# Order on a full TensorE: single score rounds, grouped head turns, later last values and new load estimates in a fused attention and mixer kernel

## The chip, the cores and the metric

The kernel runs on one core of one Trainium2 chip. The metric is the time of one execution on the device in microseconds; the profile's span is about 1.8 us shorter than the time of the same execution. A verdict calls 2% a difference. All comparisons below are between runs in the fast state, unless said otherwise. The granted clock is the share of TensorE's full clock that the trace shows as granted.

## The reference, cut to what matters

```python
def _attn_ref(q, k, v):                                   # 8 x 12 x 448 x 64 each
    scores = scale * np.matmul(q, k.transpose(0, 1, 3, 2)) - np.log(S)
    attn = 1.0 / (1.0 + np.exp(-scores))                  # sigmoid, no row sums
    return np.matmul(attn, v)

def _moe_ref(x, w_tok1, w_tok2, w_ch1, w_ch2):            # x: 8 x 448 x 768
    h = np.maximum(x.transpose(0, 2, 1) @ w_tok1, 0.0) @ w_tok2      # token mixing
    u = x + h.transpose(0, 2, 1)
    return u + np.maximum(u @ w_ch1, 0.0) @ w_ch2                    # channel mixing
```

Heads are handled in pairs of pairs: batch b has three groups m of four heads. The names in the trace are: `tk`, `tq` (the "turn", a transpose on TensorE), `qk` (a score round), `xa` (values), `xb` (turn back to x), `k` and `yn` (the two token products), `ut` (row transposes for the channel mix), `c` (the two channel products).

## The kernel before: the parts that matter

The kernel holds a small list scheduler in Python. Each piece of work is an `Op` with an engine and an estimated duration; the scheduler plays the whole program through with these estimates and emits instructions in the order it found. So a changed constant of it changes no instruction, only the order on each engine, and each engine then works through its list, and waits where an operand isn't there (at 24.44 us TensorE waited 1.06 us for a load).

```python
# the wide PSUM buffers for scores: two. The last values of batch 0 hold one of them too.
ps = plan.buf("wide", 2, [128, 2, 512], FP32, "psum", f"qk_{b}_{m}_{i}_{hs[0]}")
...
# score rounds are emitted in visits to TensorE, two rounds in each; the values of a head
# group join the fifth and the eighth visit, the last ones form a visit of their own
parts = [rs[i : i + 2] for i in range(0, len(rs), 2)]
parts[4].append(vs[0])
parts[7].append(vs[1])
groups += [(b, i / len(parts), g) for i, g in enumerate(parts)]
groups.append((b, 1.0, [vs[-1]]))
...
# when a visit is due, in us of mixer work done
return -1.0 if b < 2 else base[b - 1] - LEAD + i * SPAN * mix[b - 1]
...
# turns of batches 0 and 1 (later batches turn by DMA): one operation per head, seven
# transposes, each head into its own half of the partitions
for h in hs:
    def turn(ps=ps, h=h):
        for i, j in enumerate(ORDER[side]):
            nc.tensor.transpose(out=ps[64 * h : 64 * h + 64, i, :, :],
                                in_=raw[:, h, j, :], identity=ident[:, :])
...
# when the scheduler thinks that a load lands
free["POOL"] = 1.3
slow = 1.0 if self.pipe > 8.0 else 1.5
self.pipe = max(self.pipe, free["POOL"] + 1.5) + slow * o.us
```

From batch 2 on, x is turned by a transposing DMA: values, two copies on ScalarE, two transposing loads, then the token product of that batch. The rows of u go the same way to the channel product.

## Time and profile before

| | before |
|---|---|
| time, median (3 runs) | 384.69 us (384.46 to 387.5) |
| span of the traced run | 383.8 us |
| TensorE busy | 373.1 us, 97% |
| ScalarE / VectorE busy | 206.8 / 161.0 us |
| first channel product of batch 0 starts | 43.97 us |
| score rounds of batch 1 before it | 4 |

The prediction below shows the lines and reads them.

### The profile page before, as it was taken

What the parts mean: (1) busy time and instruction counts of PE and PEld (TensorE: products, weight loads), DVE (VectorE), ACT (ScalarE), POOL (GpSimd) and SP (SyncE); (2) the same over time, 40 slices, a digit from 0 to 9 for tenths busy, and PEclk for the clock granted to TensorE, in tenths of its full rate; (3) what the DMA queues carried; (4) which work ended last, traced back from release to release, by engine and by line L of the source; (5) the groups of instructions that cost most, each with busy time, mean ns of one, the idle gap of its engine ahead of it and who ended that gap; (6) DMA issues with size and microseconds to landing.
All of it is one profiled execution on the core that took longest, in us unless ns stands there. A gap on an engine that the chain in (4) does not pass through costs nothing.

```text
span 383.8 us, 7923 instructions
## 1 busy us (share of the span) xinstructions
PE 373.1 (97%) x3240; PEld 193.1 (50%) x3240; DVE 161.0 (42%) x296; ACT 206.8 (54%) x252; POOL 118.6 (31%) x265
## 2 busy tenths in 40 slices
PE   8989999998999999999999999999999999999995
PEld 4545544554444554444455554444445565555663
DVE  3345535355335413552341334633522264754221
ACT  2986676559757764686555665975564420200000
POOL 9973127453345423433443334344000000000000
PEclk9999999999999999999999999999999999999999
DMA  6999999979987999699797999998214463300343
GB/s 78 179 175 205 208 209 155 173 116 156 151 131 115 174 187 206 96 144 182 114 139 136 178 184 193 125 189 121 40 28 100 101 134 85 72 2 0 84 118 87
DMA packets 98804, 50.56 MB, mean 132 GB/s; under 512 B 72336, under 2 KB 95120, under 8 KB 98768
## 3 DMA queue, kind: packets, MB, share of 16 engines
q0 software_dynamic: 24400, 21.93, 42.1%
q1 hardware_dynamic: 74368, 28.13, 39.4%
q8 instruction: 25, 0.41, 0.4%
q14 instruction: 11, 0.09, 0.1%
HBM read 43.84 MB, written 11.01 MB: 143 GB/s over the span
## 4 chain that ended last, share of the span: by engine, by line
PE 87%; DMA 6%; POOL 3%; ACT 2%; DVE 1%; issue 1%; SPq 0%; POOLq 0%; ACTq 0%
PE c L861 29%; PE c L906 24%; PE qk L532 9%; PE xa L569 8%; PE yn L784 5%; PE k L754 5%; PE c L915 3%; DMA k<-in_k_dram 3%; DMA uT<-u 1%; DMA x<-xT 1%; POOL k L295 1%; POOL q L295 1%; PE k L654 1%; ACT attn L547 1%; POOL w_tok L328 1%
## 5 line engine op out<-in xcount | busy, mean ns | idle before, releaser
L547 ACT ACTIVATE attn<-qk,att_bias 128x896 f16<-128x896 f32 (+1 forms) x172 | 161.8, 988 | 75.1 <-PE qk L532 74.8
L861 PE MATMUL c<-uT,w_ch 128*128 128x448 f16 x576 | 118.1, 353 | 0.8 <-DVE uT L835 0.4
L906 PE MATMUL c<-w_ch,h2aT 128*128 128x384 f16 x576 | 98.8, 326 | 0.0
L886 DVE TENSOR_SCALAR h2aT<-c 128x448 f16<-128x448 f32 x96 | 60.0, 625 | 81.9 <-PE c L861 81.6
L861 PEld LDWEIGHTS <-w_ch 128*128 128x128 f16 x576 | 53.3, 98 | 58.0 <-issue 13.2
L906 PEld LDWEIGHTS <-h2aT 128*128 128x128 f16 x576 | 54.9, 98 | 40.9 <-issue 5.8
L930 DVE TENSOR_TENSOR u<-u,c 128x384 f32<-128x384 f32 x48 | 26.6, 555 | 79.5 <-PE c L906 79.5
L532 PE MATMUL qk<-qT,kT 64*64 64x448 f16 x672 | 52.2, 362 | 0.1
L718 POOL COPY mark<-attn 1x1 f16<-1x1 f16 x54 | 9.7, 180 | 102.9 <-ACT attn L547 102.7
L569 PE MATMUL xa<-attn,v 64*64 64x448 f16 x672 | 37.0, 351 | 0.0
L602 ACT ACTIVATE xT<-xa 128x448 f16<-128x448 f32 x43 | 21.1, 546 | 18.5 <-PE xa L569 18.0
L813 ACT ACTIVATE u<-u 128x768 f16<-128x768 f32 x21 | 17.8, 845 | 20.9 <-DVE u L805 20.8
L532 PEld LDWEIGHTS <-kT 64*64 64x64 f16 x672 | 14.5, 104 | 28.2 <-issue 24.8
L805 DVE TENSOR_TENSOR u<-x,yn 128x384 f32<-128x384 f16 x48 | 24.5, 549 | 9.9 <-PE yn L784 8.2
L784 PE MATMUL yn<-h,w_tok 128*128 128x384 f16 x128 | 26.2, 327 | 0.0
L466 POOL COPY kp<-k 128x384 f16<-128x384 f16 (+1 forms) x54 | 21.3, 431 | 14.0 <-DMA k<-in_k_dram 14.0
L569 PEld LDWEIGHTS <-v 64*64 64x64 f16 x672 | 18.7, 107 | 13.5 <-DMA q<-in_q_dram 1.5
L466 POOL COPY qp<-q 128x384 f16<-128x384 f16 (+1 forms) x54 | 21.4, 434 | 7.5 <-DMA q<-in_q_dram 7.3
L754 PE MATMUL k<-x,w_tok 128*128 128x384 f16 x112 | 20.2, 327 | 0.4 <-DMA x<-xT 0.4
L766 DVE TENSOR_SCALAR h<-k 128x384 f16<-128x384 f32 x28 | 15.6, 557 | 6.0 <-PE k L754 4.6
L784 PEld LDWEIGHTS <-w_tok 128*128 128x128 f16 x128 | 11.2, 98 | 11.7 <-issue 4.9
L306 POOL DMA_DIRECT2D k<-in_k_dram x21 | 15.1, 719 | 6.2 <-issue 5.6
(57 smaller groups left out, 192.4 us busy)
## 6 DMA issues: line engine op xcount, KB each, us to landing
out_dram<-u SPq DMA_DIRECT2D x48, 192.0 KB, 3.0
k<-in_k_dram POOLq DMA_DIRECT2D x21, 224.0 KB, 5.1
q<-in_q_dram POOLq DMA_DIRECT2D x21, 224.0 KB, 5.4
v<-in_v_dram POOLq DMA_DIRECT2D x21, 224.0 KB, 5.0
w_ch<-in_moe_w_ch_dram POOLq DMA_DIRECT2D x6, 768.0 KB, 16.2
out_dram<-ut SPq DMA_DIRECT2D x8, 192.0 KB, 3.0
v<-in_v_dram POOLq DMA_DIRECT2D x6, 112.0 KB, 4.8
x<-xT SPq DMA_TRANSPOSE x36, 4.1
```

The source lines that it names most:

```text
L466: nc.gpsimd.tensor_copy(out=pm[:, to, :, :], in_=src[:, fr, :, :])
L532: nc.tensor.matmul(out=ps[64 * s : 64 * s + 64, h, 0:S], lhsT=kT[64 * h : 64 * h + 64, i, s, :], rhs=qT[64 * h : 64 * h + 64, :, s, :], st ...
L547: nc.scalar.activation(out=at[:, hs, :], in_=ps[:, hs, 0:S], func=SIGMOID, bias=bias_t[:, :], scale=att_scale,)
L569: nc.tensor.matmul(out=ps[s](slice(64 * h, 64 * h + 64)), lhsT=vf[64 * s : 64 * s + 64, h, order[i], :], rhs=attn[i][64 * s : 64 * s + 64, ...
L602: nc.scalar.activation(out=xt[:, s, c0 : c0 + S], in_=ps[s](every), func=COPYF)
L754: nc.tensor.matmul(out=ps[:, :], lhsT=w_tok1[:, w1_slot(side, blk), 128 * t : 128 * t + 128], rhs=X[b][:, x_block(side, blk), c], start=(b ...
L784: nc.tensor.matmul(out=ps[:, :], lhsT=w_tok2[:, t, s0 : s0 + 2, :], rhs=h1[b][:, t, c], start=(t == 0), stop=(t == 1),)
L805: nc.vector.tensor_tensor(out=to, in0=x, in1=y, op=ADD)
L861: nc.tensor.matmul(out=to(), lhsT=w_ch1[cb // 4][:, db, 128 * (cb % 4) : 128 * (cb % 4) + 128], rhs=uT[b][:, db, :], start=(db == 0), stop ...
L886: nc.vector.tensor_scalar(out=h2aT[b][:, cb, :], in0=to(), scalar1=0.0, scalar2=None, op0=MAX)
L906: nc.tensor.matmul(out=ps[:, :], lhsT=h2aT[b][:, cb, 128 * blk : 128 * blk + 128], rhs=w, start=(cb == 0), stop=(cb == NCB - 1),)
L930: nc.vector.tensor_tensor(out=t, in0=t, in1=ps[:, :], op=ADD)
```

## The change

Its words are: batch 1's score rounds go one by one, not in twos; first turns in halves with heads side by side; last values of a batch join the next batch's visits. The diff also moves `LEAD` and three constants of the load model, and with the new turns the scheduler's estimate of them: 0.32 us for each head before, 0.455 for the two halves together now.

```diff
-        free["POOL"] = 1.3
+        free["POOL"] = 0.8
...
-                slow = 1.0 if self.pipe > 8.0 else 1.5
-                self.pipe = max(self.pipe, free["POOL"] + 1.5) + slow * o.us
+                slow = 1.7 if 9.0 < self.pipe < 13.0 else 1.0
+                self.pipe = max(self.pipe, free["POOL"] + 1.3) + slow * o.us
...
-    LEAD, SPAN, REST, WIDE = 12.0, 0.86, 1.0, 2
+    LEAD, SPAN, REST, WIDE = 16.0, 0.86, 1.0, 2
...
-            for h in hs:
-                def turn(ps=ps, h=h):
-                    for i, j in enumerate(ORDER[side]):
+            for a, z in ((0, 4), (4, J)):
+                def turn(ps=ps, hs=hs, a=a, z=z):
+                    for i in range(a, z):
+                        for h in hs:
...
+                if b == 1:
+                    parts = [[o] for g in parts for o in g]
+                if b >= 4:
+                    parts[1].append(left)
+                left = vs[-1]
...
-            groups.append((b, 1.0, [vs[-1]]))
+            if b == B - 1 or b < 4 - 1:
+                groups.append((b, 1.0, [vs[-1]]))
```

(A `narrow` switch in the choice of buffers is cut: it stays on, and excludes only a third wide buffer that doesn't exist.)

More of the change, by code (lines that the diff above doesn't have):

```diff
@@ L63, in __init__ @@
         self.log, self.kept = [], {}
+        self.narrow = True
         self.far, self.load_far, self.sp_wait = 4.5, 2.0, 2.0
@@ L100, in ready @@
             o = next(iter(new.values()))
-            got = sorted(
-                x for x in (self.slot_time(held, o) for held in self.slots[tag]) if x is not None
-            )
+            got = sorted(x for x, _ in self.free_slots(tag, o))
             if len(got) < len(new):
@@ L107, in ready, with free_slots @@
         return t
+    def free_slots(self, tag, o):
+        got = []
+        for i, held in enumerate(self.slots[tag]):
+            x = self.slot_time(held, o)
+            if tag == "bank" and i > 1 and not self.narrow or tag == "wide" and i == 2 and self.narrow:
+                continue
+            if tag == "wide" and i == 2 and held is None:
+                y = [self.slot_time(h, o) for h in self.slots["bank"][2:]]
+                x = None if None in y else max(y)
+            if x is not None:
+                got.append((x, i))
+        return got
     def hold(self, o):
@@ L111, in hold @@
             if b.slot is None:
-                times = [
-                    (x, i)
-                    for i, held in enumerate(self.slots[b.tag])
-                    if (x := self.slot_time(held, o)) is not None
-                ]
+                times = self.free_slots(b.tag, o)
                 b.slot = min(times)[1]
@@ L484, in turned @@
             parts = []
-            for h in hs:
-                def turn(ps=ps, h=h):
-                    for i, j in enumerate(ORDER[side]):
-                        nc.tensor.transpose(
-                            out=ps[64 * h : 64 * h + 64, i, :, :],
-                            in_=raw[:, h, j, :],
-                            identity=ident[:, :],
-                        )
-                need = [lds[h]] if len(lds) > 1 else lds
-                o = op(f"turn{what}_{b}_{m}_{h}", "PE", 0.32, turn, [*need, ident_op, *hold], [raw, ps, ident, t])
+            for a, z in ((0, 4), (4, J)):
+                def turn(ps=ps, hs=hs, a=a, z=z):
+                    for i in range(a, z):
+                        for h in hs:
+                            nc.tensor.transpose(
+                                out=ps[64 * h : 64 * h + 64, i, :, :],
+                                in_=raw[:, h, ORDER[side][i], :],
+                                identity=ident[:, :],
+                            )
+                need = [lds[hs[0]]] if len(lds) > 1 else lds
+                o = op(f"turn{what}_{b}_{m}_{hs[0]}{a}", "PE", (z - a) * 0.065, turn, [*need, ident_op, *hold], [raw, ps, ident, t])
                 o.pri = 0 if b == 0 else 2.5
```

## The prediction

> **What bounds the kernel now.** I read the busy shares first, then TensorE's timeline (start, duration, engine, instruction, count; a bracket is idle time before it and its releaser), ScalarE's timeline, and the table of waits.
>
> ```profile
> PE 373.1 (97%) x3240; PEld 193.1 (50%) x3240; DVE 161.0 (42%) x296; ACT 206.8 (54%) x252; POOL 118.6 (31%) x265
> ```
>
> TensorE is busy 97% of a 383.8 us span; nothing else passes 54%. Taken at its word, only some 10 us could be won. But "busy" here hides two things, so I went on to starts.
>
> ```profile
> 46.85 2.44 PE L861 MATMUL c<-uT,w_ch 128*128 128x448 f16 x12
> 49.22 0.57 PE L532 MATMUL qk<-qT,kT 64*64 64x448 f16 x8
> 49.73 2.44 PE L861 MATMUL c<-uT,w_ch 128*128 128x448 f16 x12
> ...
> 69.75 0.38 PE L532 MATMUL qk<-qT,kT 64*64 64x448 f16 x4
> 70.06 2.12 PE L906 MATMUL c<-w_ch,h2aT 128*128 128x384 f16 x12
> ...
> 109.38 3.58 PE L861 MATMUL c<-uT,w_ch 128*128 128x448 f16 x18
> 112.89 0.57 PE L532 MATMUL qk<-qT,kT 64*64 64x448 f16 x8
> ```
>
> The first hidden thing is the change of tile shape. From start to next start, 12 channel matmuls take 2.37 us (46.85 to 49.22) and 18 take 3.51; the difference is 0.19 us each, so a run of them carries about 0.1 us beside its matmuls. Two score rounds (x8) take 0.51, one (x4) 0.31: 0.20 a round and 0.11 fixed. Going to the 64*64 shape and back thus costs about 0.22 us, all of it inside "busy".
>
> ```profile
> 5.36 0.83 PE L443 MATMUL idle<-uT 128*128 128x256 f16 x6
> 6.12 0.58 PE L489 MATMUL tq<-ident,q 128*64 128x128 f16 x7
> ...
> 24.44 0.58 PE L489 MATMUL tk<-ident,k 128*64 128x128 f16 x7 [1.06 <-DMA k<-in_k_dram]
> ...
> 43.46 0.58 PE L489 MATMUL tq<-ident,q 128*64 128x128 f16 x7
> 43.97 2.44 PE L861 MATMUL c<-uT,w_ch 128*128 128x448 f16 x12
> ```
>
> The second is filler: the "idle" matmuls of the first 24 us do nothing but keep the engine running. So until 43.97, where the channel product of batch 0 begins, TensorE is not the bound although it looks full. Loads, ScalarE's sigmoids and short chains are. One clear loss is at 24.44: the turn of batch 1's first keys stands in TensorE's order before a score round of batch 0, and waits 1.06 us for its load.
>
> ```profile
> 29.71 2.83 ACT L547 ACTIVATE attn<-qk,att_bias 128x896 f16<-128x896 f32 x3 [0.36 <-PE qk L532]
> 33.67 0.60 ACT L636 ACTIVATE x<-xb 128x512 f16<-128x512 f16 x1 [1.13 <-DVE x L638]
> ...
> 40.35 0.54 ACT L698 ACTIVATE uT<-xa 128x448 f16<-128x448 f32 x1 [1.49 <-DVE uT L700]
> 41.06 1.91 ACT L547 ACTIVATE attn<-qk,att_bias 128x896 f16<-128x896 f32 x2 [0.16 <-PE qk L532]
> ```
>
> ScalarE ends batch 0's sigmoids at 32.54 and starts batch 1's at 41.06. Between lie 8.5 us with 3.6 us of copies: the chain values, transpose, token products of batch 0.
>
> ```profile
> 92.49 0.51 PE L826 MATMUL ut<-ident,u 128*128 128x128 f16 x6 [0.22 <-DVE u L805]
> 92.93 0.84 PE L532 MATMUL qk<-qT,kT 64*64 64x448 f16 x8
> 94.12 0.51 PE L826 MATMUL ut<-ident,u 128*128 128x128 f16 x6 [0.35 <-ACT u L813]
> 94.99 0.51 PE L826 MATMUL ut<-ident,u_tail 128*128 128x128 f16 x6 [0.35 <-ACT u_tail L813]
> 95.94 1.29 PE L861 MATMUL c<-uT,w_ch 128*128 128x448 f16 x6 [0.45 <-DVE uT L835]
> ...
> 236.88 1.47 PE L754 MATMUL k<-x,w_tok 128*128 128x384 f16 x8 [0.35 <-DMA x<-xT]
> ```
>
> At 92 to 96 TensorE has run out of batch 0's channel work and waits for batch 1's row transposes, step by step. Later only two small waits show (0.34 at 176.54 for uT, 0.35 at 236.88 for x).
>
> **What the Trainium skill says.** "Perfetto Trace Analysis", Identifying the Most-Contended Engine, calls matmul busy time a poor measure of the distance to the roof because matmuls are pipelined. The trace agrees: 97% busy, and fillers and shape changes are in it. "TensorEngine Tiling (Array Packing)", Key Properties, says that a change of tiling mode drains the engine; the 0.22 us above fits. "TensorE: Matmul & The Clock Gate", Part 3, says that tiles on different strips of the array run concurrently, and that matmuls start strictly in program order. For the first half the trace agrees: 49 transposes that follow one another from 41.26 to 42.95 take 34 ns each, 7 of one head alone take 0.51 us, 73 each. For the second half it doesn't: there q's transposes start among k's, though the program has all of k's first.
>
> **The change part by part.** I compared the order of instructions of both kernels.
>
> *Turns, heads side by side.* Six pairs of heads outside the crowd at 41.26 (k and q of batch 0's two later groups and of batch 1's first) went as 7 + 7 at 0.51 us; two streams together should take about 0.5 for all 14. That takes some 6 x 0.5 = 3 us of TensorE work, but from the filled part of the span, so it counts only as latency. In the crowd, where two streams overlap already, it gives nothing.
>
> *Fewer fillers, other places.* Before the first two q and k turns stand 4 fillers for 6; at 0.11 each (5.36 to 6.12 for six, and the 0.1 fixed) first scores move up by 0.44 us at best, as q's load allows (last issue ends at 3.68, median landing 2.4 after issue). The q turn of the second group no longer stands in front of a score round, which ended a 0.36 us gap of ScalarE. Batch 1's first k turn comes one round and 8 token matmuls later.
>
> *Score rounds of batch 1 one by one.* The last values of batch 0 hold one of two wide score buffers; a pair needs both, so none could start before 40.56. A single round fits beside. In the new order two rounds of batch 1 lie within batch 0's closing chain and five more before the first channel product: 7 instead of 4. Working the chain forward by hand with the durations above (sigmoid 1.0, casts 0.6, turn pair 0.5, load of batch 1's k still at 24.4, its last q about 41.0), last sigmoid of batch 0 ends near 32.0, the closing products near 38.1, and the first channel product starts near 42.8: 1.2 us earlier. With it lie three more rounds (3 x 0.25 = 0.75) and one token pair less (2 x 0.17 = 0.34). Net gain 1.6.
>
> *Its price.* Runs of 64*64 work number 104 for 102 in all and 77 for 76 from the first channel product on: one more there, 0.2 us lost. The pairs split are mostly made up by rounds that moved into the early part.
>
> *Row transposes of batch 1.* Batch 1's token products now come before batch 0's second channel product rather than in its middle, so 12-matmul groups of about 2 us stand between the transposes. Lost before: 0.22 + 0.35 + 0.35 + 0.45 idle, and the round at 92.93 held the engine 1.19 (to 94.12) instead of 0.51: 2.05 in all. I leave 0.4, because the first channel product of batch 1 still follows the last transpose by one pair of rounds. Gain 1.65.
>
> *Last values with the next batch's visits.* Values of batches 3 to 6 move behind the next batch's fourth round. No switch is saved: they already stood right before that batch's first pair. What goes is the pressure on the waits of 0.34 and 0.35: more channel work lies between. Gain 0.7.
>
> Sum: -1.6 - 1.65 - 0.7 + 0.2 = -3.75; I add 0.4 for new small waits of a new order: -3.35. 384.69 - 3.35 = 381.3.
>
> **The rivals.** First, single rounds as a pure price: had all ten pairs of batch 1 been split in the channel part, 10 x 0.22 = 2.2 us would go, and the time would be about 383.5. Against it speaks the count of runs. Second, the load of batch 1's first k stays at 24.4 whatever TensorE does: the turn would wait there again, ScalarE would stand for about 1 us, and the early gain would fall to some 0.4: 382.5. The DMA queues are full in these slices, so I count part of this already. Third, more: if every ScalarE gap in batch 0 (2.4 us from 12.9 to 29.7) closes, the early part gains 2.5: 379.5. Fourth, later values could make a new wait at the end: between the last token product of batch 6 and its channel product lie 7.4 us in the new order (two token groups, 12 channel matmuls and the closing 48 of 2 us each half), 9.4 before; sum, cast and transposing load took 4.4 there, so it should hold; if not, 1 to 2 us are lost: 383.
>
> **Range and chances.** The parts are certain to about 1 us each early and 0.7 in the middle. I predict 381.3 us, with 378.9 to 383.7 for 8 in 10. Over 2% faster means under 377.0, twice the gain found: 0.03. Over 2% slower would need a stall for which I see no place: 0.02. Within 2%: 0.95.
>
> **What would show it.** Right: the first channel product starts at 42 to 43.5 with seven of batch 1's score rounds before it; ScalarE has sigmoids between 33 and 40; no bracket over 0.3 us on the row transposes; no wait at the x and uT products of batches 3 and 5; turns of 14 in about 0.5 us. Wrong: a stall of over 1 us at batch 1's first k turn with the channel product still near 44, a wait of the score rounds of batch 1 on ScalarE, or a new wait on a transposing DMA at the token or channel products from batch 3 on.

## The result

| | before | after |
|---|---|---|
| time, median (range, 4 runs each) | 384.72 us (384.46 to 387.5) | 381.14 us (380.45 to 381.65) |
| span of the traced run | 383.8 us | 378.7 us |
| TensorE busy | 373.1 us (97%) | 370.8 us (98%) |
| first channel product of batch 0 | 43.97 us | 41.53 us |
| batch 1's score rounds before it | 4 | 7 |

The ratio is 0.989 (0.9841 to 0.9938): 1.1% faster, so "same" at 2%. A ratio is the mean time of one kernel's fast runs over that of the other's of the same rounds, so not quite the ratio of the medians. The two traced runs differ by 5.1 us, more than the medians (3.6), because the traced run of before took 385.59, 0.9 over its median, and the one of after 380.45, 0.7 under its own.

Where did the time come from? First the early part, TensorE's timeline of the changed kernel (start, duration, instruction, count; a bracket is idle time before it and its releaser):

```profile
12.03 0.58 PE L499 MATMUL tq<-ident,q 128*64 128x128 f16 x14
12.54 0.38 PE L542 MATMUL qk<-qT,kT 64*64 64x448 f16 x2
...
22.72 0.57 PE L542 MATMUL qk<-qT,kT 64*64 64x448 f16 x8
23.91 0.41 PE L499 MATMUL tk<-ident,k 128*64 128x128 f16 x8 [0.62 <-DMA k<-in_k_dram]
...
35.31 0.38 PE L542 MATMUL qk<-qT,kT 64*64 64x448 f16 x4
...
41.21 0.38 PE L542 MATMUL qk<-qT,kT 64*64 64x448 f16 x4
41.53 1.31 PE L871 MATMUL c<-uT,w_ch 128*128 128x448 f16 x6
```

Fourteen transposes now take 0.51 us (12.03 to 12.54). The load of batch 1's first keys is still waited for, 0.62 us, but now two score rounds of batch 0 (22.72) are already out, so ScalarE works on:

```profile
30.07 1.00 ACT L557 ACTIVATE attn<-qk,att_bias 128x896 f16<-128x896 f32 x1
...
34.20 1.00 ACT L557 ACTIVATE attn<-qk,att_bias 128x896 f16<-128x896 f32 x1
```

Batch 0's last sigmoid ends at 31.07 (before: 32.54), and batch 1's first starts at 34.20 (before: 41.06). The channel product starts 2.44 us earlier. With three more rounds done (0.25 each) and two token matmuls fewer (0.17 each) that is a lead of 2.44 + 0.75 - 0.34 = 2.85 us.

Then the row transposes of batch 1, where before had brackets of 0.22, 0.35, 0.35 and 0.45:

```profile
76.96 0.50 PE L836 MATMUL ut<-ident,u 128*128 128x128 f16 x6
77.30 0.49 PE L794 MATMUL yn<-h,w_tok 128*128 128x384 f16 x2
77.62 2.11 PE L916 MATMUL c<-w_ch,h2aT 128*128 128x384 f16 x12
...
90.54 0.50 PE L836 MATMUL ut<-ident,u_tail 128*128 128x128 f16 x6
90.97 0.57 PE L542 MATMUL qk<-qT,kT 64*64 64x448 f16 x8
91.62 2.43 PE L871 MATMUL c<-uT,w_ch 128*128 128x448 f16 x12
```

No bracket at all; groups of channel products stand between. The same by windows (a stretch of the span; its length, then TensorE, weight loads, VectorE, ScalarE, GpSimd busy, with instructions; granted clock; DMA share; GB/s), before and then after:

```profile
80.00:100.00 20.00, 18.55 (x191) 9.36 (x188) 9.75 (x19) 16.57 (x21) 9.34 (x23) 1.00 1.04 145
100.00:320.00 220.00, 219.31 (x1900) 109.91 (x1900) 88.81 (x158) 134.65 (x163) 65.41 (x156) 1.00 0.87 136
```

```profile
80.00:100.00 20.00, 19.93 (x200) 10.35 (x196) 7.90 (x15) 14.85 (x18) 7.33 (x19) 1.00 1.10 159
100.00:320.00 220.00, 220.00 (x1909) 110.75 (x1910) 89.45 (x160) 132.00 (x160) 64.12 (x153) 1.00 0.89 137
```

TensorE's idle time fell from 1.45 to 0.07 us in the first stretch, and from 0.69 to none in the long middle.

So the time came out as predicted. Whether its terms have the causes that the prediction gave them is what the experiments are for.

### The profile page after: what moved, and what is told of

Read it like the earlier page. It is cut to its first block, busy times and chain, and to the rows that moved or that the text cites. A ratio compares the mean times of both kernels' runs of the same rounds, so it can differ in the third digit from the quotient of the medians.

```text
span 378.7 us, 7932 instructions
## 1 busy us (share of the span) xinstructions
PE 370.8 (98%) x3243; PEld 191.3 (51%) x3243; DVE 160.6 (42%) x296; ACT 205.7 (54%) x252; POOL 118.5 (31%) x265
## 4 chain that ended last, share of the span: by engine, by line
PE 90%; POOL 4%; DMA 2%; ACT 1%; DVE 1%; issue 0%; POOLq 0%
PE c L871 30%; PE c L916 25%; PE qk L542 10%; PE xa L579 8%; PE yn L794 5%; PE k L764 5%; PE c L925 4%; DMA k<-in_k_dram 2%; POOL k L304 1%; POOL q L304 1%; POOL v L304 1%; ACT attn L557 1%; POOL w_tok L337 1%; PE xa L693 1%; PE tk L499 0%
## 5 line engine op out<-in xcount | busy, mean ns | idle before, releaser
L542 PE MATMUL qk<-qT,kT 64*64 64x448 f16 x672 | 53.1, 363 | 0.2 <-ACT uT L708 0.2
L794 PE MATMUL yn<-h,w_tok 128*128 128x384 f16 x128 | 27.4, 328 | 0.0
L579 PEld LDWEIGHTS <-v 64*64 64x64 f16 x672 | 19.6, 107 | 13.2 <-issue 1.6
L776 DVE TENSOR_SCALAR h<-k 128x384 f16<-128x384 f32 x28 | 15.4, 556 | 11.9 <-PE k L764 10.8
```

The source lines that it names most:

```text
L542: nc.tensor.matmul(out=ps[64 * s : 64 * s + 64, h, 0:S], lhsT=kT[64 * h : 64 * h + 64, i, s, :], rhs=qT[64 * h : 64 * h + 64, :, s, :], st ...
L579: nc.tensor.matmul(out=ps[s](slice(64 * h, 64 * h + 64)), lhsT=vf[64 * s : 64 * s + 64, h, order[i], :], rhs=attn[i][64 * s : 64 * s + 64, ...
L794: nc.tensor.matmul(out=ps[:, :], lhsT=w_tok2[:, t, s0 : s0 + 2, :], rhs=h1[b][:, t, c], start=(t == 0), stop=(t == 1),)
```

## The experiments

Twelve kernels ran. All gave the right result. Each was timed in five rounds beside the kernel before; three series on three chips. Times are lowest / median / highest of the fast runs; slow ones are named beside them.

| run | what it is | us | runs | ratio to before (95%) |
|---|---|---|---|---|
| before | three series: medians 385.54, 385.71, 385.29 | 384.32 lowest, 390.21 highest; slow: 391.12 | 127 | |
| after_again | the changed kernel | 380.77 / 380.91 / 381.46 | 4 | 0.9876 (0.9855 to 0.9898) |
| only_single | before + single rounds | 383.76 / 385.37 / 388.98 | 14 | 0.9982 (0.9951 to 1.0014) |
| undo_single | after, rounds in twos | 382.41 / 384.18 / 388.07; slow: 388.2, 388.62, 388.81 | 22 | 0.9976 (0.9949 to 1.0004) |
| head_major | after, heads not side by side | 380.69 / 380.9 / 381.14 | 4 | 0.9874 (0.9853 to 0.9895) |
| only_model | before + load constants | 383.65 / 384.45 / 385.11 | 22 | 0.9963 (0.9946 to 0.9981) |
| undo_model | after, old load constants | 381.91 / 383.03 / 386.54 | 22 | 0.9942 (0.9921 to 0.9962) |
| undo_turn | after, old turns | 381.81 / 382.11 / 383.45 | 8 | 0.9912 (0.9882 to 0.9943) |
| undo_join | after, last values alone | 380.84 / 381.76 / 384.71 | 10 | 0.9896 (0.9863 to 0.9929) |
| only_join | before + join | 384.29 / 384.96 / 386.16; slow: 2099.11 | 22 | 0.9986 (0.9969 to 1.0004) |
| undo_lead | after, LEAD 12 | 379.97 / 380.83 / 382.1 | 6 | 0.9871 (0.9833 to 0.9909) |
| load_swap | after, batch 1's loads earlier | 380.82 / 380.96 / 381.1 | 4 | 0.9875 (0.9836 to 0.9915) |
| more_single | after + single rounds in batches 3, 5 | 382.82 / 384.05 / 386.59; slow: 2087.23 | 22 | 0.9957 (0.9941 to 0.9972) |

My first theory was the prediction's: the single rounds carry the early gain and the row transposes. The rival was that the turns do.

To compare early parts, I take the start of the first channel product and subtract what TensorE had already done of later work: 0.25 us for each of batch 1's rounds before it and 0.17 for each second token matmul. For before that is 43.97 - 4 x 0.25 - 6 x 0.17 = 41.95; for after 41.53 - 7 x 0.25 - 4 x 0.17 = 39.10.

| trace | channel product | rounds, matmuls done | early mark | end of batch 0's last sigmoid | closing stretch |
|---|---|---|---|---|---|
| before | 43.97 | 4, 6 | 41.95 | 32.54 | 9.41 |
| only_single | 45.45 | 8, 4 | 42.77 | 32.48 | 10.29 |
| only_model | 42.32 | 4, 6 | 40.30 | 31.27 | 9.03 |
| undo_single | 40.70 | 2, 6 | 39.18 | 31.17 | 8.01 |
| undo_model | 43.03 | 7, 4 | 40.60 | 31.44 | 9.16 |
| undo_turn | 43.59 | 8, 4 | 40.91 | 31.54 | 9.37 |
| after, after_again, head_major, load_swap | 41.53, 42.56, 42.02, 42.18 | 7, 4 | 39.10, 40.13, 39.59, 39.75 | 31.07, 32.09, 31.48, 31.72 | 8.03, 8.04, 8.11, 8.03 |
| undo_join, undo_lead, more_single | 42.28, 42.32, 42.97 | 7, 4 | 39.85, 39.89, 40.54 | 31.82, 31.70, 32.51 | 8.03, 8.19, 8.03 |

The seven traces of the last two rows have the same order of TensorE work up to the channel product. Their marks lie 1.4 us apart, as their loads land, so a difference of marks under that says nothing. The mark is steadier when it is cut in two where ScalarE ends batch 0's last sigmoid. The spread is in the first part (31.07 to 32.51). The rest, the closing stretch (mark less end of sigmoid), is 8.03 to 8.19 in all seven, and 9.41 in before.

### The changed kernel again

> The changed kernel once more, for the spread. Both theories: 381.1 us within 0.6; the first channel product starts at 41 to 42.5 us, the row transposes of batch 1 show no idle bracket over 0.3 us. The wait of the first k turn of batch 1 (0.62 us in the first trace) may differ by 0.5 us with the load's landing.

380.91 us, span 379.7, channel product at 42.56, the k wait 0.46. As expected; the spread is 0.7 us, against 5.8 for before in the same series (384.43 to 390.19, 35 runs). The steadiness itself was not expected.

### Single rounds alone

```diff
 # on the kernel before
                 parts[7].append(vs[1])
+                if b == 1:
+                    parts = [[o] for g in parts for o in g]
```

> The kernel before with batch 1's score rounds one by one and nothing else of the change. Theory (single rounds carry the gain, since one of them fits beside the last values that hold a wide buffer, and the earlier end of batch 1 pulls its token products ahead of the second channel product): 381.9 us, 381.2 to 382.8, first channel product near 42.5 to 43, no waits at the row transposes. Rival (the turns side by side carry it, single rounds only cost switches): 384.5 or more.

The theory missed: median 385.37, no clear gain, and the channel product at 45.45 with eight rounds before it, an early mark 0.8 us later than before's and a closing stretch 0.9 longer. So in this trace the rounds put into batch 0's closing chain were not free, and bought nothing. But the second half of the theory held: the row transposes show no wait. What took the place of that gain stands in the trace, TensorE's timeline:

```profile
193.80 1.47 PE L754 MATMUL k<-x,w_tok 128*128 128x384 f16 x8 [1.30 <-DMA x<-xT]
236.83 2.21 PE L754 MATMUL k<-x,w_tok 128*128 128x384 f16 x8 [2.27 <-DMA x<-xT]
```

Two token products waited 3.6 us for their x. The second cost more than its wait: its eight matmuls took 2.21 us instead of 1.47. The windows tell why (granted clock is the third number from the end):

```profile
232.00:236.00 4.00, 2.56 (x26) 1.09 (x21) 1.18 (x2) 1.91 (x2) 1.05 (x3) 1.00 1.10 171
236.00:240.00 4.00, 3.17 (x17) 1.16 (x17) 1.12 (x2) 0.39 (x1) 1.56 (x4) 0.67 1.07 191
240.00:244.00 4.00, 4.00 (x26) 1.84 (x25) 1.85 (x4) 2.17 (x3) 2.08 (x5) 0.90 0.15 34
```

In the 4 us from 236, the first 0.83 of them still in the wait, the granted clock averaged 0.67, and 0.90 in the next 4. The trace's own clock record has 0.50 for 3.41 us from 237.39. This traced run (388.98 us) is the longest of its 14, all of which count as fast.

### Rounds in twos again

```diff
 # on the changed kernel
-                if b == 1:
-                    parts = [[o] for g in parts for o in g]
```

> The changed kernel with batch 1's rounds in twos again. Theory: most of the gain is lost, 383.5 to 385.5 us; waits at the row transposes are back (1 to 2.5 us in all). Rival (turns carry it): 381.5 to 382.3.

As the theory said by time: 384.18, and the lowest, 382.41, is 1.6 above that of after_again. But the early mark is 39.18 and the closing stretch 8.01, as good as any of the changed kernel's. The early gain doesn't come from the single rounds. What is lost stands later:

```profile
87.64 0.51 PE L836 MATMUL ut<-ident,u 128*128 128x128 f16 x6 [0.22 <-ACT u L823]
88.37 0.51 PE L836 MATMUL ut<-ident,u 128*128 128x128 f16 x6 [0.22 <-ACT u L823]
141.76 1.29 PE L871 MATMUL c<-uT,w_ch 128*128 128x448 f16 x6 [1.92 <-DMA uT<-u]
```

The row transposes wait again, but 0.44 us in all and not the 1 to 2.5 expected, and a new wait of 1.92 us stands at batch 2's channel product. Between batch 2's last token product and that point lie 6.0 us of matmuls here and 10.3 in the changed kernel (counted from the order, 0.19 us for each 448-column matmul, 0.16 for 384, 0.08 for each 128 by 64 one, 0.05 for each 64 by 64 one). In this trace 6.0 was too short for the sum, cast and transposing load.

### Side by side or one head after the other

```diff
 # on the changed kernel; the order of all groups stays
-                    for i in range(a, z):
-                        for h in hs:
+                    for h in hs:
+                        for i in range(a, z):
```

> The changed kernel, the same order of all groups, but within each half turn one head's transposes first and then the other's. Both theories: an 8 or 6 group takes clearly longer than 0.36 us, 14 alone 0.7 to 1.0 instead of 0.51. Theory (the early part is not bound by TensorE): 0 to 0.6 us over the changed kernel, 381.1 to 381.7. Rival (side by side carries the gain): 2 to 3 us lost, 383 to 384.

The time, 380.9, is as the theory said. The duration was missed by both:

```profile
12.03 0.59 PE L499 MATMUL tq<-ident,q 128*64 128x128 f16 x14
12.55 0.38 PE L542 MATMUL qk<-qT,kT 64*64 64x448 f16 x2
```

0.52 us for 14, against 0.51 side by side. With four and three transposes of one head at a time the order within the group does nothing. The two heads write to different halves of the partitions, and the starts in the trace come in pairs 13 ns apart with 56 ns to the next pair: two streams run together. Old turns, seven of one head and then seven of the other, gain two thirds of this too where nothing stands between them; only_model's trace has such a pair, 0.69 us for 14:

```profile
21.83 0.75 PE L489 MATMUL tq<-ident,q 128*64 128x128 f16 x14
22.52 0.28 PE L443 MATMUL idle<-uT 128*128 128x256 f16 x1
```

So what counts most is that no other shape stands between the two sevens (7 and 7 apart take 0.51 each).

### The load constants, alone and undone

```diff
 # only_model: these three lines on the kernel before; undo_model: the reverse on the changed one
+        free["POOL"] = 0.8
+                slow = 1.7 if 9.0 < self.pipe < 13.0 else 1.0
+                self.pipe = max(self.pipe, free["POOL"] + 1.3) + slow * o.us
```

> The kernel before with nothing but the scheduler's new estimates of when the early loads land (three constants of the diff). Theory M (these estimates, not the turns or the single rounds, gave the early gain, by keeping turns that wait for loads from standing in front of score rounds): first channel product at 42 to 42.8 us with 4 rounds before it, as against 43.97; fastest runs 382.6 to 383.6, still with a tail to 386 or more. Theory T (the turns side by side give it): first channel product at 43.5 to 44.3, fastest runs 384 to 384.6.

> The changed kernel with the scheduler's old estimates of early loads. Theory M: the first channel product comes 1.5 to 2.5 us later, 382.3 to 383.5 us. Theory T: within 0.5 us of the changed kernel, 380.8 to 381.5.

With the single rounds fallen as the early cause, this was the new theory, M. Alone, the constants give an early mark of 40.30, 1.65 better than before, and the lowest time, 383.65, is 0.8 under before's. From the first channel product on, TensorE's order in this trace is that of before, group for group, so the clear gain (0.9963) comes from a change of order before it. The expected tail did not come: no run is above 385.11, and 39 of before's 49 in that series are. Undone, the mark is 40.60, just outside the range of the seven traces, and the median rises by 2.1 us to 383.03; some of the later order moves with it, so not all of that need be early. No load lands earlier for it by intent: the constants move turns that wait for loads behind score rounds whose operands are there. M holds for a part, with the turns' share still to find.

### The old turns

```diff
 # on the changed kernel
-            for a, z in ((0, 4), (4, J)):
+            for h in hs:          # (cut) one operation of seven transposes per head, as before
```

> The changed kernel with the old turns: one head's seven after the other's. Theory M: 381 to 381.8 us, the first channel product within 0.6 us of 42 once eight rounds instead of seven before it are counted. Theory T: 382.5 to 384 us.

382.11 median, 1.2 above the changed kernel: between the two theories' ranges. The mark is 40.91, 0.4 beyond the range of the seven traces, though no load is waited for in this one. The closing stretch is clearer. New constants with old turns give 9.03 (only_model) and 9.37 (here), new turns with old constants 9.16 (undo_model), before had 9.41, and only both together give 8.01 to 8.19. So about 1.4 us of the early gain need both: turns of two heads in one group and the place that the constants give them. What is gained before the last sigmoid, 0 to 1.5 us, is within the spread of the loads. The new turns alone, on the kernel before, were not run.

### The last values, undone and alone

```diff
 # undo_join, on the changed kernel; only_join is the reverse on the kernel before
-                if b >= 4:
-                    parts[1].append(left)
-                left = vs[-1]
-            if b == B - 1 or b < 4 - 1:
-                groups.append((b, 1.0, [vs[-1]]))
+            groups.append((b, 1.0, [vs[-1]]))
```

> The changed kernel with the last values of batches 3 to 6 alone again. Theory J (the join takes the token products of the next batch further from the values whose transposing load they wait for; it removes waits that vary from run to run): fastest runs within 0.5 us of the changed kernel, but a spread of over 2 us, and in some traces a wait of 0.3 to 2.5 us on x at a token product at 190 or 235. Rival (the join does nothing, spread comes from elsewhere): 380.7 to 381.5 for all runs.

> The kernel before with the last values of batches 3 to 6 joined to the next batch's visits and nothing else. Between these values and the token product that needs them lie 8.1, 8.1, 11.0 and 6.4 us of matmul work instead of 6.8, 5.3, 5.8 and 5.3. Theory J: no wait on x at a token product near 190 or 235, fastest runs 0.3 to 0.9 us under those of before (384.4), and no run above 386. Rival (the join is idle, the tail has another cause): 384.4 to 390 as before.

Undone: lowest 380.84, as the changed kernel; median 381.76, highest 384.71. Its trace has the wait back:

```profile
233.07 1.48 PE L764 MATMUL k<-x,w_tok 128*128 128x384 f16 x8 [0.40 <-DMA x<-xT]
```

Alone: the lowest, 384.29, is as before's (384.32 in that series), so the expected 0.3 to 0.9 us at the fast end is a miss; that before's fastest runs don't have these waits is a guess. The long end is nearly as expected: highest 386.16, where before had 13 of 43 runs above 386.2, up to 391.12 (that one slow). By the mean this is not clear (0.9986, interval up to 1.0004). So the join gives no speed to a good run, and bad runs were fewer with it. That the distance does this is not shown, and two kernels speak against it: only_model has no join and before's order of these products, a wait of 1.02 us on x in its trace (at 233.85), and no run above 385.11; undo_single has the join, and fast runs up to 388.07. What makes the tail stays open. The one run of 2099.11 us was the traced one, and that trace was not used: in it a channel matmul took 1524 ns instead of 353. The view of that trace gives a granted clock of 1.000, but its clock record is empty, where all the others have entries, so this says nothing of the clock. more_single had one such run too, of 2087.23. Both are marked slow and stand outside the verdicts; their cause is open.

### The lead

```diff
-    LEAD, SPAN, REST, WIDE = 16.0, 0.86, 1.0, 2
+    LEAD, SPAN, REST, WIDE = 12.0, 0.86, 1.0, 2
```

> The changed kernel with the lead at 12 again instead of 16. Only the last batch's distance falls (13.7 to 5.8 us between its last values and its token product). Theory J: 380.8 to 382, at most one small wait on x near 305. Rival (the lead gives the middle its gain): 382.5 or more.

380.83: nothing is lost. The lead gives no time that these runs show. Its lowest run, 379.97, is the fastest of the study, but six runs that reach 382.1 don't make it a better version.

### Batch 1's loads earlier

```diff
-    tok1_late = load_w_tok1(1)
     ch1_ld, ch2_ld = [], []
     load_all(1, 0)
+    tok1_late = load_w_tok1(1)
```

> The changed kernel with batch 1's first key, query and value loads issued ahead of the late part of the token weights. If the wait at batch 1's first k turn (0.62 us, or hidden in the landing's jitter) is on the path: 0.3 to 1.0 us faster than the changed kernel, 380.0 to 380.6. Rival (another load or ScalarE sets the early end): 380.7 to 381.3.

Batch 1's first keys land at 22.76, where the two traces of the changed kernel have 23.87 and 24.89. The wait at their turn is gone, and the time is 380.96, the changed kernel's. So this wait is worth nothing that the runs show. Other waits remain in this stage. The same trace has a bracket of 1.02 us on an earlier k load; the swap did not make it, since the same load was waited for 0.55 us in after_again and 0.89 in head_major:

```profile
18.50 0.58 PE L499 MATMUL tk<-ident,k 128*64 128x128 f16 x14 [1.02 <-DMA k<-in_k_dram]
```

### The price of a single round

```diff
-                if b == 1:
+                if b in (1, 3, 5):
                     parts = [[o] for g in parts for o in g]
                 if b >= 4:
-                    parts[1].append(left)
+                    parts[3 if b == 5 else 1].append(left)
```

> The changed kernel with the rounds of batches 3 and 5 one by one too: 86 runs of 64 by 64 work from the first channel product on instead of 77, the distances to the waiting products nearly the same. Theory (a run costs about 0.22 us of drain wherever TensorE is the bound): 2.0 us slower than the changed kernel, 382.4 to 383.6. Rival (the fixed cost of a run is hidden): within 0.5 us of it.

384.05, 3.1 above the changed kernel where 2.0 was expected for nine more runs of 64 by 64 work. The direction is clear, and the rival (hidden cost) falls. The size isn't pure: its trace, of the longest fast run (386.59), also has waits of 0.79 us on uT, 0.81 on x and 0.44 on uT. The 0.81 stands 10.8 us after the end of the values that the product needs (146.73 to 157.53), more than the 6.6 (133.29 to 139.84, read the same way) that were too short for uT in undo_single; the load was issued at 151.28 and landed at 158.20. So distance doesn't explain all of these waits; what makes the transposing loads late in one run and not in another stays open.

## Why the prediction was right or wrong

The time (381.3 predicted, 381.14 measured) and the range were right. That they fit so well is partly luck: errors of the terms cancel, and the fall of 3.35 us, close to the 3.6 between the first four runs of each, was 4.6 between the medians of the longer series (385.54 and 380.91). Of the terms:

- **Turns.** Right that 14 take about 0.5 us (0.51). Wrong in the reason: heads need not alternate one by one (0.52 without, 0.69 with seven and seven); grouping does most.
- **Fillers and places.** "First scores move up by 0.44 us at best": they moved from 7.90 to 7.61. The places of the turns, which the prediction named but gave no number of their own, turned out to be a main part of the early gain, together with the grouping.
- **Score rounds one by one, -1.6.** This is the step that failed. The chain worked out by hand did end early (2.85 us between the two traces, 1.4 to 2.85 over seven traces of the same order), but the prediction put the whole gain under the single rounds ("none could start before 40.56"; "7 instead of 4"). The rounds did move, 7 of them, yet taking them back left the closing stretch at 8.01, and adding them alone left it at 10.29 (before 9.41). The early gain that is clear of the loads' spread, 1.4 us, comes from turns in one group in the places that the load constants give them; the hand-walk had used those durations and that order without crediting them. The product came at 41.53, earlier than the 42 to 43.5 given as the sign of being right; six further traces of this order have 42.02 to 42.97.
- **Its price, +0.2.** One more run from the first channel product on; nine more in more_single cost 3.1 us, waits included, so a cost of that order or somewhat more per run.
- **Row transposes, -1.65.** Right in size and in direction: 1.45 us of idle became 0.07 between 80 and 100 us, and the transposes' waits are absent with single rounds alone. Undoing only these brought back 0.44 of the 1.37 us of brackets, so they are not the whole cause. The working has a slip: the 1.19 us from 92.93 to 94.12 contain the bracket of 0.35 already, so 1.70 were lost and not 2.05. No wait was left over, so the 0.4 held back made the slip good, which is luck.
- **Last values, -0.7.** Right that "what goes is the pressure on the waits", and both waits (0.34 and 0.35) are gone. Mis-sized as a fixed term: alone the join gives about 0 in a fast run, and what it is worth in a bad one is open. With the join undone no wait on uT came back, and 0.40 on x did. That before has a tail to 390 us was not foreseen, because only three runs were to be seen.
- **New small waits, +0.4.** None showed in the changed kernel's two traces after the closing stretch.

Of the rivals, the single rounds as a pure price came out true for single rounds alone (0.9982), for another reason than the one given: later waits for x. The pinned load did stay (0.62 us of waiting), but taking it away gained nothing. The third, more, came true in part: between 12.9 us and the end of batch 0's sigmoids, ScalarE's gaps fell from 2.42 to 1.02 us in the two traces. Its 379.5 doesn't follow from its 2.5, which in place of 1.6 gives 380.4. The fourth, a new wait at the end, did not come. The parts don't add up: alone, single rounds, constants and join give 0.1 to 0.4%, and two of the three are not clear of nothing; together with the turns they give 1.2%. The closing stretch shows one such pair (9.03 to 9.37 with one of turns and constants, 8.03 with both). For the rest, that each part removes a wait that another's gain would run into is argued, not shown.

No version beat the changed kernel clearly.

## What to carry to other kernels

On an engine that is full, look at where an instruction that may wait stands in its order: move it behind work that is ready, and keep work of one tile shape together. Before shortening a path, count the independent work that hides each transposing load behind it, in microseconds, and keep it well above the load's slow case (6.6 us were too short once here, and 10.8 once); one trace doesn't show the tail. Test each part of a change both alone and undone: a sum can come out right with its terms under the wrong names.

## What the Trainium skill lacked or had wrong

- "TensorE: Matmul & The Clock Gate", Part 3, says that matmuls start strictly in program order. Transposes of 64 output columns didn't: in the kernel before q's start among k's from 41.68 us on, and 14 issued in fours and threes of one head take 0.52 us, as side by side (0.51), where seven alone take 0.51.
- "TensorEngine Tiling (Array Packing)", Key Properties, says that a mode switch drains but gives no cost. Here there and back is about 0.22 us (0.11 us fixed in a score run, 0.1 in the run it interrupts); nine more such runs came to 3.1 us, with some waits in it.
- "TensorE: Matmul & The Clock Gate", Part 1, speaks of an idle window of about 3.4 us before the clock falls. A single wait of 2.27 us was followed by a granted clock of 0.50 for 3.4 us, and eight matmuls took 2.21 us instead of 1.47; one of 1.92 us in undo_single left the clock at 1.00.
- No page that I found tells how far waits for transposing loads vary. At one pair of token products before's trace waited 0.35 us on x and only_model's 1.02, with TensorE's order the same from the first channel product on. Fast runs of before took 384.32 to 390.21 us, those of the changed kernel 380.45 to 381.65.
- "TensorE: Matmul & The Clock Gate", Part 1, warns that clock events in a trace can be wrong and that the gate was seen stuck at a quarter for over 50 us. No page that I found tells of a whole execution like that: in the run of 2099.11 us matmuls took some four times as long (1524 ns for 353), and its clock record is empty. Whether it was the gate is not shown.
